# dV and dK stores of two attention backward passes: from GpSimd's DMA queue to SyncE's, in a fixed order with the K and V loads

## The chip, the cores and the metric

The kernel runs on one core of one Trainium2 chip, in bfloat16 with float32 accumulation. The metric is the device time of one execution in microseconds (us). Engines are called as the profile calls them: PE (TensorE), PEld (its weight loads), DVE (VectorE), ACT (ScalarE), POOL (GpSimd), SP (SyncE, which here only issues DMAs).

## The reference

Two independent attention blocks A and B, each with its own inputs, and the gradients of all of them for a given grad_out; the two outputs lie side by side in the last dimension.

```python
B, Sq, D = x.shape                     # 8, 96, 640
H, Dh = 32, 128                        # k_cache, v_cache: 8 x 32 x 512 x 128
q = (x @ wq).reshape(B, Sq, H, Dh).transpose(0, 2, 1, 3)
scores = einsum("bhqd,bhkd->bhqk", q, k_cache) * (Dh ** -0.5)
p = softmax(scores, axis=-1)
o = einsum("bhqk,bhkd->bhqd", p, v_cache)
out = o.transpose(0, 2, 1, 3).reshape(B, Sq, H * Dh) @ wo
...
# returned: out (A and B concatenated), then dx, dK, dV, dwq, dwo of A and of B
```

dK and dV have the size of the caches: 8 x 32 x 512 x 128 each, 33.5 MB, so four such outputs of 134.2 MB in all are written, and as much is read.

## The kernel before

The work goes in ticks. One tick starts one batch entry b of one head h of one block, so there are 2 x 32 x 8 = 512 of them, about 3.3 us each. What one (h, b) needs is spread over some 14 ticks as a software pipeline written out by hand: `em.add(tick, slot, function)` collects the pieces, they are sorted by tick and slot, and then recorded in that order. OFF gives the tick of each piece relative to the entry's own tick, SLOTS the place within a tick:

```python
OFF = dict(ldk=-5, ldv=-3, kt=-3, vt=0, s2=3, s3=3, s4=4, s5=5, s6=6, s7=7, s8=8)
SLOTS = dict(LOAD=0, S2A=5, S2B=5.5, S1=6, S8=10, S7=20, S5=30, S4=40, S6=50, S3A=52, S3B=53, S5B=54, HEAD=SL_HEAD, GRP=SL_GRP)
```

A scheduler of the language then may still move instructions on their engine by its own estimate, unless an instruction is wrapped in `pinned` (`tc.keep_in_program_order`): pinned instructions of one engine keep the recorded order among themselves.

The pieces around the change:

- `c_ld` (L262 to L270) loads K or V of two batch entries (a pair) at once, 256 KB, from SP. K_sb has 7 such buffers, V_sb 5. Not pinned.
- `c_xt` (L272 to L278) transposes such a pair on the way from SBUF to SBUF with a DMA transpose, also from SP: VT for every pair (4 buffers), KT for every second pair (2 buffers). For the other pairs PE transposes K itself (`c_s1`, L285). Not pinned.
- `c_s2a`, `c_s2b`, `c_s3a`, `c_s3b`: scores on PE (S_ps, L298), row maximum on DVE (L300), exponential on ACT (E_sb, L310), 1/sum on DVE (rinv, L320), product P_sb on POOL (L329, pinned).
- `c_s4` (L382 to L393): dV = P^T dO on PE (dV_ps, L389), evicted by ACT into dV_sb (L392), which holds two ticks and has 3 buffers. `c_s7` (L425 to L436): the same for dK (dK_ps L432, dK_sb L435).
- `c_st` (L395 to L399): when both ticks of a pair are evicted, one store of 256 KB from dV_sb or dK_sb to the output, issued from POOL and pinned there, one tick after the product, behind that tick's P_sb and prod.
- `c_s6` (L411): dP = dO V^T on PE, reading VT (L417), and dS on DVE (L421). `c_s8` and `c_s45` (L333 to L380): dQ, the transposes of dS and P, and O, with evictions by ACT (L375, L378).

Every eighth tick a head begins and another ends: its weights wq and wo are loaded from POOL (L190, L199), its projections are made on PE (L243) and its dwq and dwo are made and stored from POOL (L474, L496). After each group of up to 6 heads the partial out and dx are summed (`gU`, L512). At the border of A and B, x and grad_out of B are loaded from SP (ld_tmp, L118) and transposed on PE (L134).

Of the kernel before, what the change touches and what calls it, by code (L numbers as in the profile page):

```python
# [44 lines left out]
OFF = dict(ldk=-5, ldv=-3, kt=-3, vt=0, s2=3, s3=3, s4=4, s5=5, s6=6, s7=7, s8=8)  # L45
# [5 lines left out]
SLOTS = dict(LOAD=0, S2A=5, S2B=5.5, S1=6, S8=10, S7=20, S5=30, S4=40, S6=50, S3A=52, S3B=53, S5B=54, HEAD=SL_HEAD, GRP=SL_GRP)  # L51


def build_block(tc, em, tick0, blk, x, kc, vc, wq, wo, g_all, out_all, dx, dk, dv, dwq, dwo, ident, ones, pools, HG=6, first=True, groups=None):
    nc = tc.nc
# [7 lines left out]
    KC = Sk // 128  # L63
    NB = 2
# [38 lines left out]
    SB = {}  # L103
    HS = pools["HS"]
    CS = pools["CS"]
# [5 lines left out]
    def pinned(ins):  # L111
        return tc.keep_in_program_order(ins)
# [68 lines left out]
    def pA(h):  # L181
        def f():
            start = first and h == 0
            if h % 2 == 0:
                wq_p = hd.tile([128, DC, 256], BF16, name="wq_p", bufs=2)
                with nc.allow_non_contiguous_dma(reason="wq slice of two heads"):
                    if start:
                        nc.sync.dma_start(wq_p[:], wq_v[:, :, h * 128:(h + 2) * 128])
                    else:
                        pinned(nc.gpsimd.dma_start(wq_p[:], wq_v[:, :, h * 128:(h + 2) * 128]))  # L190
            else:
                wq_p = HS[(blk, h - 1)]["wq_p"]
            HS[(blk, h)] = dict(wq_p=wq_p, wq_h=wq_p[:, :, (h % 2) * 128:(h % 2 + 1) * 128])
        return f

    def pA2(h):
        def f():
            wo_h = hst.tile([128, D], BF16, name="wo_h", bufs=HG + 3)
            ld = nc.gpsimd.dma_start(wo_h[:], wo[h * 128:(h + 1) * 128, :])  # L199
            if not (first and h == 0):  # L200
                pinned(ld)
            HS[(blk, h)]["wo_h"] = wo_h
        return f
# [23 lines left out]
    def pC(h, which, si):  # L227
        def f():
            st = HS[(blk, h)]
            (t0, w) = tsplits[si]  # L230
            if which == 0:
                dst = st["QT_h"]
                lhs = lambda c: st["wq_h"][:, c, :]
                rhsT = S["xT"]
                sc = scale
            else:
                dst = st["dOT_h"]
                lhs = lambda c: st["woT_h"][:, c * 128:(c + 1) * 128]
                rhsT = S["gT"]
                sc = None  # L240
            q_ps = bank([128, w], F32, "q_ps")
            for c in range(DC):
                nc.tensor.matmul(q_ps[:], lhs(c), rhsT[:, c, t0:t0 + w], start=(c == 0), stop=(c == DC - 1))  # L243
            evac(EV["pC%d%d" % (which, si)], dst[:, t0:t0 + w], q_ps[:], sc)
        return f
# [16 lines left out]
    def c_ld(h, b, n, bufs):  # L262
        def f():
            src = kc if n == "K" else vc
            X = kvp.tile([128, NB, KC, 128], BF16, name=n + "_sb", bufs=bufs)
            nc.sync.dma_start(X[:], src[b:b + NB, h].rearrange("b (p c) d -> p b c d", c=KC))
            for i in range(NB):
                st = CS.setdefault((blk, h, b + i), {})
                st[n + "_sb"], st[n + "_all"] = X[:, i], X
        return f  # L270

    def c_xt(h, b, name, bufs):  # L272
        def f():
            XT = kvp.tile([128, NB * KC, 128], BF16, name=name, bufs=bufs)
            nc.sync.dma_start_transpose(XT[:], CS[(blk, h, b)][name[0] + "_all"][:].rearrange("p a c d -> p (a c d)"))
            for i in range(NB):
                CS[(blk, h, b + i)][name] = XT[:, i * KC:(i + 1) * KC].rearrange("p c k -> p (c k)")
        return f  # L278
# [116 lines left out]
    def c_st(h, b, which):  # L395
        def f():
            dst = dv if which == "v" else dk
            pinned(nc.gpsimd.dma_start(dst[b - 1:b + 1, h].rearrange("b (p c) d -> p b (c d)", c=KC), SB.pop((blk, h, b // 2, which))[:]))  # L398
        return f  # L399

    def c_s5b(h, b):
# [146 lines left out]
    def k_on_pe(h, b):  # L548
        return (b // NB) % 2 == 0 or h == 0 or (first and h == 1)

    SX = pools["SX"]
    for g in range(NG):
        h0 = GH0[g]
        for hh in range(groups[g]):
            h = h0 + hh
            c0t = tick0 + h * B
            if not (first and h == 0):
                em.add(c0t + HK["pA"], 54.6, pA(h))
                em.add(c0t + HK["pA2"], 54.6, pA2(h))
            em.add(c0t + HK["pB"], SL_HEAD, pB(h))  # L560
            fh = first and h == 0
            p0, p1, d1, d0, late = HK["pC0"], HK["pC1"], HK["pD1"], HK["pD0"], 0
            if fh:
                p1, d1, d0, late = [3, 3], 3, 4, 7
            elif h == 0:
                p0, p1, d1, d0, late = [-2, 2], [0, 3], 3, 4, 7
            for si in range(NTS):
                em.add(c0t + p0[min(si, 1)], SL_HEAD, pC(h, 0, si))
                em.add(c0t + p1[min(si, 1)], SL_HEAD + late, pC(h, 1, si))
            em.add(c0t + d1, SL_HEAD + (8 if late else 0), pD(h, 1))  # L570
            em.add(c0t + d0, SL_HEAD, pD(h, 0))
            for b in range(B):
                ct = c0t + b
                if b % NB == 0:
                    em.add(tick0 - 12 if first and h == 0 and b == 0 else ct + OFF["ldk"], SLOTS["LOAD"], c_ld(h, b, "K", 7))
                    em.add(ct + OFF["ldv"], SLOTS["LOAD"], c_ld(h, b, "V", 5))
                    if not k_on_pe(h, b):
                        em.add(ct + OFF["kt"], SLOTS["LOAD"] + 1, c_xt(h, b, "KT", 2))
                    em.add(ct + OFF["vt"], SLOTS["LOAD"] + 1, c_xt(h, b, "VT", 4))
                if k_on_pe(h, b):  # L580
                    em.add(ct + 2, SLOTS["S1"], c_s1(h, b))
                em.add(ct + OFF["s2"], SLOTS["S2A"], c_s2a(h, b))
                em.add(ct + OFF["s2"], SLOTS["S2B"], c_s2b(h, b))
                em.add(ct + OFF["s3"], SLOTS["S3A"], c_s3a(h, b))
                em.add(ct + OFF["s3"], SLOTS["S3B"], c_s3b(h, b))
                em.add(ct + OFF["s5"], SLOTS["S5B"], c_s5b(h, b))
                if b % 2 == 1:
                    em.add(ct + OFF["s4"] + 1, 54.3, c_st(h, b, "v"))
                    em.add(ct + OFF["s7"] + 1, 54.3, c_st(h, b, "k"))
                em.add(ct + OFF["s4"], SLOTS["S4"], c_s4(h, b))  # L590
                for i, o in enumerate(("s8", "s7", "s5", "s4")):
                    SX.setdefault(ct + OFF[o], [None] * 4)[i] = (blk, h, b)
                em.add(ct + OFF["s6"], SLOTS["S6"], c_s6(h, b))
                em.add(ct + OFF["s7"], SLOTS["S7"], c_s7(h, b))
            hk = HK if first or h < H - 1 else dict(HK, qA0=13, qB=[14, 15], qA1=16, qD=[(19, 0, 2), (19, 2, 4), (19, 4, 5)])
            em.add(c0t + hk["qA0"], SL_HEAD, qA(h, 0))
            for di in range(len(wsplits)):
                em.add(c0t + hk["qB"][di], SL_HEAD + 1, qB(h, di))
            em.add(c0t + hk["qA1"], SL_HEAD, qA(h, 1))
            for (k_, c_lo, c_hi) in hk["qD"]:  # L600
                if c_lo < DC and h % 2 == 1:
                    em.add(c0t + k_, SL_HEAD + 2, qD(h, c_lo, min(c_hi, DC)))
        cLg = tick0 + (h0 + groups[g] - 1) * B + B - 1
        gs0 = max(3, (GSPREAD0 * groups[g]) // HG)
        gs1 = max(3, (GSPREAD1 * groups[g]) // HG)
        if not first and g == NG - 2:
            gs0, gs1 = 9, 9
        if g == 0:
            em.add(cLg + OFF["s5"] - 2, SL_LOAD, setup_acc)
        subs = [(0, t, gi) for t in range(TT) for gi in range(len(gsplits))] + [(1, t, gi) for t in range(TT) for gi in range(len(gsplits))]  # L610
        n_out = TT * len(gsplits)
        for i, (which, t, gi) in enumerate(subs):
            if which == 0:
                tk = cLg + OFF["s5"] + 2 + (i * gs0) // n_out
            else:
                tk = cLg + OFF["s8"] + 2 + gs0 - 3 + ((i - n_out) * gs1) // n_out
            em.add(tk, SL_GRP, gU(g, which, t, gi))
# [124 lines left out]
```

## Time and profile before

| | |
|---|---|
| runs, median of 3 | 1705.34 us (1693.32 to 1706.98) |
| profiled execution, span from first to last instruction | 1699.8 us |
| PE busy | 1675.7 us (99%) |
| ACT, DVE, POOL busy | 1405.2, 1329.8, 1040.3 us |
| SP's queue (q1) | 242.08 MB in 546576 packets |
| POOL's queue (q0) | 177.35 MB in 53584 packets |
| stores of dV, of dK (POOL, L398) | 256 each, mean 761 and 762 ns on POOL; 5.2 and 5.3 us to landing |
| loads of K and V (SP, L266) | 512, 5.2 us to landing |
| transposes by DMA (SP, L275) | 256 of V, 122 of K, 5.8 us to landing |

Of the profiled execution the page gives the span, and no time from outside it; it lies within the range of the three runs. Busy time of an engine is the time in which it executes; for POOL it includes the issue of its DMAs, while all of SP's instructions count as issue or wait. "To landing" is the median from issue to the completion of the transfer. The share of a DMA queue is the time that its packets took, over 16 engines' span; packets of two queues on one engine can overlap in it, so shares can add to more than 100%.

### The profile page before, as it was taken

The page shows a single profiled execution, that of the slowest core. Times are in us where ns is not written, and L with a number is a line of the kernel's source. Part 1 is how long each engine was busy: PE and PEld are TensorE (multiplying, and loading weights), DVE is VectorE, ACT ScalarE, POOL GpSimd, SP SyncE. Part 2 cuts the span into 40 slices and gives each one's busy share as a digit, 9 for nine tenths or more (in the row PEclk, how much of TensorE's full clock was granted, in tenths as well). Part 3 has the DMA queues.
Part 4 walks back from the last instruction along what each step waited for, and adds up shares of the span by engine and source line. Part 5 has one row for each costly group of instructions (what it writes and reads, how often), then busy time and mean ns, then how long its engine had stood idle before and what let it go on. Part 6 is the DMA issues. An engine that isn't in the chain of part 4 may idle for free.

```text
span 1699.8 us, 56567 instructions
## 1 busy us (share of the span) xinstructions
PE 1675.7 (99%) x22024; PEld 1343.8 (79%) x22024; DVE 1329.8 (78%) x3052; ACT 1405.2 (83%) x3518; POOL 1040.3 (61%) x1747
## 2 busy tenths in 40 slices
PE   8999999999999999999999999999999999999999
PEld 7877778778778778777778877887788778778876
DVE  6887678878788878787778876787788778878877
ACT  6998889869869869878768998897799679878975
POOL 3676567646647647656566764675576557656754
PEclk9999999999999999999999999999999999999999
DMA  9999999999999999999999999999899989999994
GB/s 256 252 259 250 258 225 260 262 242 243 262 221 252 268 238 259 225 251 237 281 256 269 273 270 248 238 289 248 218 261 276 237 221 261 281 217 240 263 247 141
DMA packets 600429, 423.05 MB, mean 249 GB/s; under 512 B 419360, under 2 KB 557984, under 8 KB 600160
## 3 DMA queue, kind: packets, MB, share of 16 engines
q1 hardware_dynamic: 546576, 242.08, 72.2%
q0 software_dynamic: 53584, 177.35, 32.7%
q8 instruction: 173, 2.83, 0.7%
q14 instruction: 96, 0.79, 0.2%
HBM read 161.09 MB, written 159.12 MB: 188 GB/s over the span
## 4 chain that ended last, share of the span: by engine, by line
PE 89%; DMA 4%; ACT 3%; issue 1%; DVE 1%; POOL 0%; SPq 0%; DVEq 0%; ACTq 0%; POOLq 0%
PE q_ps L243 12%; PE o_ps L512 12%; PE dwo_ps L470 6%; PE dV_ps L389 6%; PE dK_ps L432 6%; PE S_ps L298 6%; PE dP_ps L417 6%; PE dwq_ps L490 6%; PE x_ps L340 5%; PE x_ps L365 5%; PE dst_ps L346 5%; PE x_ps L359 5%; PE kT_ps L285 3%; PE n_ps L258 3%; PE nat_ps L455 2%; DMA VT<-V_sb 1%
## 5 line engine op out<-in xcount | busy, mean ns | idle before, releaser
L329 POOL TENSOR_SCALAR P_sb<-E_sb,rinv 96x512 bf16<-96x512 bf16 x512 | 352.6, 689 | 567.8 <-DVE rinv L320 559.2
L310 ACT ACTIVATE E_sb<-S_ps,negm 96x512 bf16<-96x512 f32 x512 | 351.0, 686 | 187.6 <-DVE negm L300 181.9
L421 DVE SCALAR_TENSOR_TENSOR dS_sb<-dP_ps,dl_ps,P_sb 96x512 bf16<-96x512 f32 x512 | 382.1, 746 | 60.9 <-PE dl_ps L419 54.6
L300 DVE TENSOR_REDUCE negm<-S_ps 96x1 f32<-96x512 f32 x512 | 347.6, 679 | 50.9 <-PE S_ps L298 46.6
L435 ACT ACTIVATE dK_sb<-dK_ps 128x512 bf16<-128x512 f32 x512 | 302.1, 590 | 63.4 <-PE dK_ps L432 56.5
L392 ACT ACTIVATE dV_sb<-dV_ps 128x512 bf16<-128x512 f32 x512 | 311.6, 609 | 0.0
L378 ACT ACTIVATE PT_sb<-x_ps 128x384 bf16<-128x384 bf16 x512 | 253.1, 494 | 0.0
L512 PEld LDWEIGHTS <-OD 128*128 128x128 bf16 x1536 | 132.2, 98 | 100.4 <-issue 1.0
L398 POOL DMA_DIRECT2D out_dram<-dV_sb x256 | 194.9, 761 | 11.8 <-issue 8.6
L398 POOL DMA_DIRECT2D out_dram<-dK_sb x256 | 195.0, 762 | 9.1 <-issue 4.4
L389 PE MATMUL dV_ps<-dOnat_h,P_sb 96*128 96x128 bf16 x2048 | 198.2, 219 | 0.8 <-DVE dOnat_h L160 0.6
L417 PE MATMUL dP_ps<-VT,dOT_h 128*96 128x512 bf16 x512 | 195.4, 382 | 3.0 <-DMA VT<-V_sb 3.0
L432 PE MATMUL dK_ps<-Qnat_h,dS_sb 96*128 96x128 bf16 x2048 | 198.1, 219 | 0.1
L407 POOL TENSOR_TENSOR prod<-OD,dOT_h 128x96 bf16<-128x96 bf16 x512 | 184.2, 360 | 13.8 <-ACT OD L375 12.6
L348 DVE COPY dST_sb<-dst_ps 128x384 bf16<-128x384 bf16 x512 | 177.1, 346 | 10.5 <-PE dst_ps L346 10.3
L365 PE MATMUL x_ps<-ident,P_sb 96*128 96x96 bf16 x2048 | 172.0, 205 | 0.8 <-POOL P_sb L329 0.3
L359 PE MATMUL x_ps<-PT_sb,V_sb 128*128 128x96 bf16 x2048 | 172.3, 206 | 0.2 <-ACT PT_sb L378 0.2
L346 PE MATMUL dst_ps<-ident,dS_sb 96*128 96x96 bf16 x2048 | 172.3, 206 | 0.2 <-DVE dS_sb L421 0.2
L340 PE MATMUL x_ps<-dST_sb,K_sb 128*128 128x96 bf16 x2048 | 171.0, 206 | 1.3 <-ACT dK_sb L435 0.8
L375 ACT ACTIVATE OD<-x_ps 128x192 bf16<-128x192 f32 (+1 forms) x515 | 167.9, 326 | 3.9 <-PE x_ps L340 3.9
L320 DVE RECIPROCAL rinv<-rowsum 96x1 f32<-96x1 f32 x512 | 79.9, 156 | 106.0 <-ACT E_sb L310 100.4
L340 PEld LDWEIGHTS <-K_sb 128*128 128x128 bf16 x2048 | 131.1, 98 | 25.1 <-issue 1.6
(84 smaller groups left out, 3744.4 us busy)
## 6 DMA issues: line engine op xcount, KB each, us to landing
out_dram<-dV_sb POOLq DMA_DIRECT2D x256, 256.0 KB, 5.2
out_dram<-dK_sb POOLq DMA_DIRECT2D x256, 256.0 KB, 5.3
K_sb<-in_A_k_cache_dram SPq DMA_DIRECT2D x128, 256.0 KB, 5.3
V_sb<-in_A_v_cache_dram SPq DMA_DIRECT2D x128, 256.0 KB, 5.2
K_sb<-in_B_k_cache_dram SPq DMA_DIRECT2D x128, 256.0 KB, 5.0
V_sb<-in_B_v_cache_dram SPq DMA_DIRECT2D x128, 256.0 KB, 4.9
out_dram<-dwo_sb POOLq DMA_DIRECT2D x63, 160.0 KB, 4.8
out_dram<-dwq_sb POOLq DMA_DIRECT2D x31, 320.0 KB, 6.1
```

The source lines that it names most:

```text
L300: nc.vector.tensor_reduce(negm[:], S_ps[:], axis=AX.X, op=ALU.max, negate=True)
L310: nc.scalar.activation(E_sb[:], st["S_ps"][:], ACT.Exp, bias=st["negm"][:], scale=1.0, accum_out=rowsum[:])
L329: pinned(nc.gpsimd.tensor_scalar(P_sb[:], st["E_sb"][:], st["rinv"][:], 0.0, op0=ALU.mult, op1=ALU.add))
L340: nc.tensor.matmul(dQT_ps, st["K_sb"][:, c, :], st["dST_sb"][:, c * Sq:(c + 1) * Sq], start=(c == 0), stop=(c == KC - 1))
L389: nc.tensor.matmul(dV_ps[:, c * 128:(c + 1) * 128], P_sb[:, c * 128:(c + 1) * 128], hs["dOnat_h"][:, b * 128:(b + 1) * 128], start=True, s ...
L392: nc.scalar.activation(SB[(blk, h, b // 2, "v")][:, b % 2], dV_ps[:], ACT.Identity, scale=1.0)
L398: pinned(nc.gpsimd.dma_start(dst[b - 1:b + 1, h].rearrange("b (p c) d -> p b (c d)", c=KC), SB.pop((blk, h, b // 2, which))[:]))
L417: nc.tensor.matmul(dP_ps[:], hs["dOT_h"][:, tok], st["VT"], start=True, stop=True)
L421: nc.vector.scalar_tensor_tensor(dS_sb[:], dP_ps[:], dl_ps[:, 0:1], st["P_sb"][:], op0=ALU.subtract, op1=ALU.mult)
L432: nc.tensor.matmul(dK_ps[:, c * 128:(c + 1) * 128], dS_sb[:, c * 128:(c + 1) * 128], hs["Qnat_h"][:, b * 128:(b + 1) * 128], start=True, s ...
L435: nc.scalar.activation(SB[(blk, h, b // 2, "k")][:, b % 2], dK_ps[:], ACT.Identity, scale=1.0)
L512: nc.tensor.matmul(o_ps[:], src[:, t * 128:(t + 1) * 128], rhs, start=(hh == 0), stop=(hh == groups[g] - 1))
```

## The change

The stores of dV and dK are issued from SP. Their slot moves from 54.3 (late in the tick) to 1.5, behind the tick's loads (0) and DMA transposes (1) and ahead of the compute, still one tick after the product. The K and V loads and the transposes are pinned as well, so that SP issues all of these in the recorded order: in one tick V, K, KT (every second pair) and the store of dK, in the next VT and the store of dV.

```diff
@@ c_ld
-            nc.sync.dma_start(X[:], src[b:b + NB, h].rearrange("b (p c) d -> p b c d", c=KC))
+            pinned(nc.sync.dma_start(X[:], src[b:b + NB, h].rearrange("b (p c) d -> p b c d", c=KC)))
@@ c_xt
-            nc.sync.dma_start_transpose(XT[:], CS[(blk, h, b)][name[0] + "_all"][:].rearrange("p a c d -> p (a c d)"))
+            pinned(nc.sync.dma_start_transpose(XT[:], CS[(blk, h, b)][name[0] + "_all"][:].rearrange("p a c d -> p (a c d)")))
@@ c_st
-            pinned(nc.gpsimd.dma_start(dst[b - 1:b + 1, h].rearrange("b (p c) d -> p b (c d)", c=KC), SB.pop((blk, h, b // 2, which))[:]))
+            pinned(nc.sync.dma_start(dst[b - 1:b + 1, h].rearrange("b (p c) d -> p b (c d)", c=KC), SB.pop((blk, h, b // 2, which))[:]))
@@ build_block
                 if b % 2 == 1:
-                    em.add(ct + OFF["s4"] + 1, 54.3, c_st(h, b, "v"))
-                    em.add(ct + OFF["s7"] + 1, 54.3, c_st(h, b, "k"))
+                    em.add(ct + OFF["s4"] + 1, SLOTS["LOAD"] + 1.5, c_st(h, b, "v"))
+                    em.add(ct + OFF["s7"] + 1, SLOTS["LOAD"] + 1.5, c_st(h, b, "k"))
```

In the built programs the order on PE, DVE and ACT is the same as before. On SP the K transpose stood before directly behind the load that feeds it; now it stands behind the next pair's loads. The compiler gives each DMA of SP one of eight completion semaphores in turn, before and after, and a DMA waits until the earlier one on its semaphore has landed.

## The prediction

> **What bounds the kernel now.** I read the engine totals first, then what TensorE (PE) waited for, then the DMA queues and the same totals by stage, and last SyncE's (SP's) waits. From the page:
>
> ```profile
> span 1699.8 us, 56567 instructions
> PE 1675.7 (99%) x22024; PEld 1343.8 (79%) x22024; DVE 1329.8 (78%) x3052; ACT 1405.2 (83%) x3518; POOL 1040.3 (61%) x1747
> ```
>
> PE is busy in 1675.7 of 1699.8 us, so 24.1 us is all the idle time that any change around it can remove. The instruction order of the changed program is the same as before on PE, VectorE and ScalarE; GpSimd (POOL) loses 512 DMA issues and SP gains them. PE's work therefore stays 1675.7 us and only its idle time can move. What that idle time waits for, by the view of PE's waits:
>
> ```profile
> PE dP_ps L417 <- DMA VT<-V_sb: 3.0, 2, 2.4
> PE tp_ps L134 <- DMA ld_tmp<-in_grad_out_dram: 2.7, 1, 2.7
> PE S_ps L298 <- DMA KT<-K_sb: 2.1, 1, 2.1
> PE kT_ps L285 <- ACT dK_sb L435: 1.6, 1, 1.6
> ```
>
> Columns: us in total, times, longest. All DMA waits are a few us, so the transfers are hidden today. The DMA queues of the page show at what margin:
>
> ```profile
> q1 hardware_dynamic: 546576, 242.08, 72.2%
> q0 software_dynamic: 53584, 177.35, 32.7%
> ```
>
> Packets, MB, share of 16 engines' span. q1 is SP's queue (loads and transposes), q0 POOL's (stores, weights). They add to 104.9%: there is hardly a moment without packets in flight, though over 100% says that packets of the two queues overlap, so the share is not pure work. The view by stages (PE, PEld, DVE, ACT, POOL busy, granted clock, DMA share, GB/s):
>
> ```profile
> 250.00:350.00 100.00, 99.75 (x1338) 80.89 (x1336) 80.94 (x186) 86.84 (x218) 65.05 (x111) 1.00 1.14 256
> 650.00:750.00 100.00, 99.31 (x1319) 79.49 (x1317) 80.74 (x186) 83.01 (x209) 62.68 (x105) 1.00 1.14 240
> 1150.00:1250.00 100.00, 99.62 (x1267) 78.12 (x1265) 77.87 (x181) 76.83 (x191) 56.72 (x95) 1.00 0.96 236
> ```
>
> Of the sixteen 100 us stages from 50 to 1650 us, seven have a DMA share of 1.11 or more, the lowest has 0.96. PE is the bound, and DMA is a close second, kept off the path by prefetch. Pairing each V transpose with the dP matmul that reads it (k-th transpose, matmul 2k-1), it lands 11.9 us ahead in the median, but 2.7 us or less ahead in one of twenty, mostly near 100 to 170, 690 to 730 and 970 to 1010 us. That reserve is what the change draws on or refills.
>
> **What leaves POOL.** 512 issues of 0.76 us (page, L398: 194.9 + 195.0 us). POOL falls to about 650 us. POOL's P_sb (L329) waits 559.2 us for rinv in 404 of 512 cases, so in most ticks it was idle when its input came, and PE waits for P_sb 0.3 us in all (2.0 us at its weight loads). Value: 0, bounds 0 and -2 us. What hides the lost 390 us is that idle time itself: POOL was no bound.
>
> **What SP gains.** I price a store's issue by the K and V loads on the same queue, which have the same size and shape (128 partitions, 256 KB): medians 474 to 615 ns, mean of the four 0.53 us, so 512 x 0.53 = 271 us. SP issues today 512 x 0.53 + 256 x 1.44 (V transposes) + 122 x 1.25 (K) = 793 us, later 1064 us, 63% of the span. A pair of ticks takes (1669.2 - 12.2) / 256 = 6.5 us (first and last S_ps matmul); per pair SP then issues for 4.2 us. It fits, with 2.3 us for waits, where it had 3.4.
>
> **The waits on SP.** Each store waits for ScalarE's eviction of the tick before. Behind it in the order stand the V transpose or the next pair's loads. Those wait themselves for PE work of the tick before to free a buffer, so a store's wait ends about when theirs do: value 0; bounds 0 and, for a dV store that comes after the eviction ending a tick, the 0.6 us of that eviction (L392) x 256 = 154 us on SP, spent from the reserve above and not on PE. In exchange the fixed order takes this away:
>
> ```profile
> SPq L266 <- PE dK_ps L432: 180.0, 102, 4.2
> SPq L275 <- DMA K_sb<-in_A_k_cache_dram: 169.4, 57, 9.0
> SPq L275 <- DMA K_sb<-in_B_k_cache_dram: 152.0, 61, 4.8
> ```
>
> Today a K transpose stands right behind the load that feeds it and blocks SP until that lands, 321 us in 118 waits. In the new order it stands two ticks later, behind the next pair's loads, and a store parts it from the V transpose. So loads behind it leave earlier. There is one more wait: the program has eight completion semaphores for SP's DMAs, taken in turn, so a DMA must have landed before the eighth one after it is issued. Per pair SP had 890 / 256 = 3.5 DMAs and will have 5.5: the limit moves from 15 us to 8 / 5.5 x 6.5 = 9.5 us. Landing medians are 5.2 (loads, L266) and 5.8 us (transposes, L275); the longest are 14.4 and 14.9, so it binds in the crowded stages only.
>
> **The transfers.** The bytes stay, the packets change. q0 averages 177.35 MB / 53584 = 3.3 KB a packet; the packets between 512 B and 2 KB, 557984 - 419360 = 138,624 by the page, are SP's plain DMAs, about 256 of 1 KB for each of 512 loads, and a store from SP has the same rows. The tail of the trace has each kind alone, stores from POOL in 1676 to 1686 us and stores from SP in 1686.5 to 1699.8 us:
>
> ```profile
> q0 software_dynamic: 368, 1.21, 31.7%
> ```
>
> ```profile
> q1 hardware_dynamic: 2528, 2.46, 53.2%
> ```
>
> 0.317 x 10 x 16 = 50.7 engine-us for 1.21 MB, 41.9 ns per KB; 0.532 x 13.3 x 16 = 113.2 for 2.46 MB, 46.0 ns per KB. The 512 stores carry 134.2 MB: 4.1 ns x 134,200 / 16 = 34 us more on all sixteen engines. It reaches the path only where DMA has no room: 7 of 16 stages, 15 us. Bounds: 0 (prefetch takes it all) and 34 us, plus what is lost if one queue cannot overlap transfers as two do, at most the 4.9% above 100%, 83 us.
>
> [...]
>
> **The gain.** With K's landing out of SP's way, the PE waits for VT (3.0) and KT (2.1) and the two behind a store's landing (1.6 above, 0.8 at L340) can go: 7.5 us. Bounds: 0 and the whole 24.1 us. I take 7.5, since the blocking that makes loads late is removed everywhere.
>
> **The sum.** 1699.8 + 15 - 7.5 = 1707.3 us. The page gives the profiled execution's span and no other time for it; the span lies 5.5 us under the median of the runs (1705.34; 1693.32 to 1706.98), so I put the 7.5 us on the median: 1713 us, +0.4%. Runs of this kernel lie 0.8% apart, so about 1% is what a measurement can tell from no change.
>
> **Rivals.**
>
> *Slower: the store's landing holds ScalarE.* dV_sb and dK_sb have three buffers of two ticks. A pair's buffer is stored in the third tick and written again in the seventh, four ticks or 13 us later. The trace has this happening once, after a late landing:
>
> ```profile
> 794.86 0.60 ACT L435 ACTIVATE dK_sb<-dK_ps 128x512 bf16<-128x512 f32 x1 [1.79 <-DMA out_dram<-dK_sb]
> ```
>
> ```profile
> 795.50 0.38 PE L285 MATMUL kT_ps<-ident,K_sb 128*128 128x128 bf16 x4 [1.65 <-ACT dK_sb L435]
> ```
>
> ScalarE waits 1.79 us for the store of that buffer and PE loses 1.65. In the new order a store also queues behind transposes and loads, on SP and in the ring. If one ring serves 34 us more work and loses half of the overlap (41 us), with the 7.5 us gain not coming, that is +75, 1780. If only the seven crowded stages pay and the gain still comes, 75 x 7 / 16 - 7.5 = +25, 1731. Centre 1755. It decides once a store lands more than 13 us after its eviction in the seven crowded stages. For: 1.11 to 1.14 shares there, landings up to 14.9 us. Against: only two such waits on ScalarE now (3.1 us), landing median 5.3.
>
> *Faster: the ring gets smoother.* A store from SP in the tail lands 1.8 us after issue (160 KB), from POOL 2.5 at least (256 KB). If packets cost the same in traffic, the 34 us vanish and most of the 24.1 us idle goes, less what start and end keep: about -18, 1687. For: no more K-landing block. Against: PE's waits for VT, KT and ld_tmp are only 8.7 us (3.0, 2.1, 2.7 and 0.9).
>
> *Nothing moves.* That stores stay on POOL is ruled out by the built order; that both effects hide wholly gives 1705.
>
> **Chances.** Forecast (within 1%, nothing moving included) 0.43; slower rival 0.40; faster rival 0.17. The range takes 1684 (3 us short of losing all 24.1 us) to 1768, midway between the slower rival's centre and its upper end; the forecast's own is 1697 to 1722.
>
> **What would show it.** Right: PE busy near 1676; POOL near 650; q0 down to about 43 MB and q1 up to 376 MB with some 131,000 more packets; the K_sb row gone from SP's waits; a few us in "ACT <- DMA out_dram". Wrong: tens of us in that row or in S_ps and dP_ps on KT and VT (slower), or PE idle under 10 us (faster).

## The result, and the profile after

| | before | after |
|---|---|---|
| median of the runs, us | 1704.81 (15 runs, 1692.10 to 1717.71) | 1685.62 (15 runs, 1683.96 to 1688.83) |
| ratio, 95% interval | | 0.9893 [0.9869, 0.9917] |
| profiled execution, span | 1699.8 | 1682.2 (its own time 1683.96) |
| PE busy, idle in the span | 1675.7, 24.1 | 1669.7, 12.5 |

The changed kernel is 1.1% faster. The forecast was +0.4%, within 1%. Ratios, here and below, are taken over all fast runs, those within 1.5% of the fastest of their kernel, so they differ a little from the quotient of two medians.

The totals of the page after, first the engines, then the two DMA queues (packets, MB, share of 16 engines' span):

```profile
span 1682.2 us, 57193 instructions
PE 1669.7 (99%) x22024; PEld 1340.7 (80%) x22024; DVE 1329.0 (79%) x3052; ACT 1403.0 (83%) x3518; POOL 665.7 (40%) x1235
...
q1 hardware_dynamic: 685840, 376.33, 93.1%
q0 software_dynamic: 12624, 43.10, 7.9%
```

The 17.6 us that the span lost are 11.6 us less idle time and 6.0 us less busy time on PE, with the same 22024 matmuls. The bytes moved as forecast, and q1 has 139,264 packets more (131,000 forecast). The queues' shares add to 101.0%, where they were 104.9%.

The longest of PE's waits after (us in total, times, longest):

```profile
PE warm_ps L658 <- DVE warm L645: 1.1, 1, 1.1
PE q_ps L243 <- ACT gT L157: 0.6, 1, 0.6
PE dV_ps L389 <- DVE dOnat_h L160: 0.6, 1, 0.6
PE q_ps L243 <- DVE gT L160: 0.6, 1, 0.6
```

All four rows shown of before are gone: VT, ld_tmp, KT, and ScalarE's dK_sb. Between 20 and 1650 us, PE idled 16.4 us before and 5.0 us after; some 7.5 us lie at the start and the end in both. The three stages that were shown before:

```profile
250.00:350.00 100.00, 99.89 (x1331) 80.45 (x1330) 79.84 (x184) 84.77 (x214) 40.90 (x76) 1.00 1.06 260
...
650.00:750.00 100.00, 99.94 (x1323) 79.76 (x1322) 81.63 (x189) 82.90 (x209) 40.05 (x74) 1.00 1.03 256
...
1150.00:1250.00 100.00, 99.64 (x1301) 79.58 (x1298) 78.98 (x181) 78.24 (x196) 35.92 (x67) 1.00 0.96 227
```

The DMA share, last column but one, fell from 1.14 to 1.06 and 1.03 in two of these stages. It did not fall everywhere: the highest of the sixteen stages is 1.14 after too (50 to 150 us, 1.13 before). SP's waits after:

```profile
SPq L266 <- PE dK_ps L432: 312.8, 165, 4.6
...
SPq L398 <- ACT dV_sb L392: 46.3, 91, 3.7
...
SPq L398 <- ACT PT_sb L378: 36.2, 76, 1.3
```

The K_sb rows (321 us) are down to 1.6 us. The stores (L398) wait for ScalarE instead. The first row of the K and V loads (L266) grew from 180.0 us; all their waits for PE together grew little, from 464 to 488 us. How the V transposes land is at the end of the view of the tile VT, before and then after:

```profile
DMA to landing us min/median/max: 3.1/6.1/14.9
```

```profile
DMA to landing us min/median/max: 3.1/4.9/10.4
```

Pairing each of the 378 transposes in the trace with the first matmul that reads it gives the reserve (landed so long before use). Before, it is under 3 us for 33 of them and zero for the worst; after, for none, with 3.7 us the least.

**Why busy time fell too.** This is the first late V transpose of before in PE's timeline (start, us, instruction, and in brackets the wait ahead of it), then the stretch behind it by windows (us, busy PE, PEld, DVE, ACT, POOL, granted clock, DMA share, GB/s):

```profile
125.33 0.39 PE L417 MATMUL dP_ps<-VT,dOT_h 128*96 128x512 bf16 x1 [2.37 <-DMA VT<-V_sb]
...
126.81 2.55 PE L490 MATMUL dwq_ps<-dQnat,x_nat 128*128 128x256 bf16 x11
```

```profile
127.00:128.00 1.00, 1.00 (x7) 0.73 (x5) 0.85 (x2) 0.05 (x1) 0.00 (x0) 0.50 1.08 262
...
130.00:131.00 1.00, 1.00 (x23) 1.00 (x21) 0.74 (x4) 0.46 (x1) 0.40 (x1) 1.00 0.85 59
...
829.00:833.00 4.00, 4.00 (x43) 3.38 (x42) 2.46 (x7) 2.46 (x6) 1.73 (x3) 0.59 1.15 251
```

PE waits 2.37 us, then runs at a granted clock of 0.50 from 126.6 to 130.0 us. The wait for ld_tmp (2.74 us) at 826 us was followed by 3.4 us of half clock as well (0.59 in the mean from 829 to 833 us). So these two waits are paid twice: their 6.8 us at half clock cost PE about 3.4 us of the 6.0 (an estimate, half of 6.8). The trace of after has none of it between 20 and 1650 us. Instruction by instruction (the order is the same), 1.8 us of the 6.0 lie from 100 to 150 us, 1.7 from 800 to 850 and 1.4 in the first 50 us; the last are not explained.

So late transposes are not all of the 17.6 us. They account for 5.1 us of waits (VT 3.0, KT 2.1) and about 1.7 us of half clock; x and grad_out of B (ld_tmp) for 3.6 us (2.7 and 0.9) and 1.7; ScalarE's buffers, held by stores, for 2.4 (1.6 and 0.8). What they share is a transfer that lands late.

One profiled execution is one of many, but the record has the mean granted clock of every run. Of the 97 runs of before beside the experiments, the 4 with 1.000 took 1695.9 us in the mean, the 24 with 0.998 took 1703.4 and the 16 with 0.995 took 1713.4 (correlation of time and clock over all 97: -0.75). All 15 runs of after had 0.999 or 1.000. So the scatter of before goes with half clock that differs from run to run, but even its runs at full clock are some 10 us slower than after.

### The profile page after: what moved, and what is told of

Read it like the earlier page. It is cut to its first block, busy times and chain, and to the rows that moved or that the text cites. A ratio compares the mean times of both kernels' runs of the same rounds, so it can differ in the third digit from the quotient of the medians.

```text
span 1682.2 us, 57193 instructions
## 1 busy us (share of the span) xinstructions
PE 1669.7 (99%) x22024; PEld 1340.7 (80%) x22024; DVE 1329.0 (79%) x3052; ACT 1403.0 (83%) x3518; POOL 665.7 (40%) x1235
## 4 chain that ended last, share of the span: by engine, by line
PE 93%; ACT 3%; DVE 1%; issue 1%; DMA 1%; POOL 0%; SPq 0%; DVEq 0%; ACTq 0%; POOLq 0%
PE q_ps L243 13%; PE o_ps L512 12%; PE dwo_ps L470 7%; PE dK_ps L432 6%; PE dV_ps L389 6%; PE S_ps L298 6%; PE dwq_ps L490 6%; PE dP_ps L417 6%; PE x_ps L340 5%; PE dst_ps L346 5%; PE x_ps L365 5%; PE x_ps L359 5%; PE kT_ps L285 3%; PE n_ps L258 3%; PE nat_ps L455 2%
## 5 line engine op out<-in xcount | busy, mean ns | idle before, releaser
L359 PE MATMUL x_ps<-PT_sb,V_sb 128*128 128x96 bf16 x2048 | 172.1, 206 | 0.5 <-ACT PT_sb L378 0.5
L243 PE MATMUL q_ps<-gT,woT_h 128*128 128x512 bf16 (+1 forms) x640 | 136.9, 325 | 1.2 <-ACT gT L157 0.6
L470 PE MATMUL dwo_ps<-g_nat,Onat 128*128 128x320 bf16 x768 | 135.2, 298 | 1.6 <-ACT E_sb L310 0.2
```

## Experiments

All times are ratios to runs of the kernel before on the same chip. "DMA time" is the sum of the queues' shares (q0, q1 and, in e7, ScalarE's q10) times the span; "reserve < 3" counts transposes; "K wait" is SP's wait for a K load to land (L275 on K_sb). The last three are worked out from one profiled execution. Those of after, e1 and e6 are among the fastest of their kernel (1683.96, 1719.71 and 1685.65 us).

| kernel | stores on | median, us | ratio [95%] | DMA time, us | reserve < 3 | K wait, us |
|---|---|---|---|---|---|---|
| before | POOL | 1704.81 | 1 | 1783 | 33 | 321 |
| after | SP | 1685.62 | 0.9893 [0.9869, 0.9917] | 1699 | 0 | 2 |
| e1 pins only | POOL | 1727.34 | 1.0128 [1.0096, 1.0161] | 1793 | 24 | 116 |
| e2 stores only | SP | 1687.49 | 0.9891 [0.9867, 0.9914] | 1752 | 0 | 95 |
| e4 POOL kept busy | SP | 1688.05 | 0.9893 [0.9872, 0.9915] | 1700 | 0 | 3 |
| e5 dV only | half | 1687.08 | 0.9866 [0.9831, 0.9901] | 1735 | 2 | 47 |
| e6 dK only | half | 1691.08 | 0.9927 [0.9896, 0.9959] | 1723 | 0 | 18 |
| e9 pins, KT early | POOL | 1709.66 | 0.9975 [0.9941, 1.0009] | 1775 | 29 | 329 |
| e11 all earlier | POOL | 1715.24 | 1.0035 [0.9997, 1.0072] | 1694 | 15 | 44 |
| e13 K and KT early | POOL | 1738.30 | 1.0162 [1.0115, 1.0210] | 1810 | 34 | 0 |
| e14 K and KT early | SP | 1685.82 | 0.9888 [0.9856, 0.9920] | 1732 | 0 | 0 |
| e3 KT early | SP | 1708.87 | 1.0018 [0.9992, 1.0043] | 1780 | 0 | 180 |
| e8 e3, dK_sb x4 | SP | 1710.45 | 1.0006 [0.9977, 1.0036] | 1788 | 0 | 183 |
| e10 e8, dV_sb x4, V_sb x4 | SP | 1715.49 | 1.0053 [1.0019, 1.0086] | 1808 | 73 | 201 |
| e12 e3, store first | SP | 1694.85 | 0.9923 [0.9892, 0.9955] | 1761 | 0 | 162 |
| e7 stores on ScalarE | ACT | 1797.74 | one run | 1735 | – | 11 |

### Queue, order or POOL's time: e1, e2, e4

After reading the two traces there were three theories: A, the fixed order (SP no longer blocked by K landings); B, the queue of the stores (their place in the tick moves with it); C, POOL's 390 us.

e1 undoes the move of the stores and keeps the pins:

```diff
-            pinned(nc.sync.dma_start(dst[b - 1:b + 1, h]...
+            pinned(nc.gpsimd.dma_start(dst[b - 1:b + 1, h]...
-                    em.add(ct + OFF["s4"] + 1, SLOTS["LOAD"] + 1.5, c_st(h, b, "v"))   # and dK alike
+                    em.add(ct + OFF["s4"] + 1, 54.3, c_st(h, b, "v"))
```

> The K and V loads and the DMA transposes are pinned in the fixed order on SP as in the change; the stores of dV and dK stay on POOL as before. Theory A (order): the gain comes from taking the K transpose away from behind its own load, where it blocked SP for 321 us in 118 waits; then this alone gives most of the gain, 1684 to 1692 us, and the waits of SP for K_sb's landing are gone. Theory B (queue): the gain comes from the stores leaving POOL's queue, since transfers of two queues disturb each other; then this stays at 1698 to 1706 us, with PE still waiting a few us for VT or KT. In either theory POOL stays near 1040 us.

e2 moves the stores and leaves loads and transposes unpinned:

```diff
-            pinned(nc.sync.dma_start(X[:], src[...]))     # c_ld; c_xt alike
+            nc.sync.dma_start(X[:], src[...])
```

> The stores go to SP as in the change, but loads and transposes are not pinned, so the scheduler orders them against the pinned stores by its own estimate; the K transpose stands one load nearer to its own K load than in the change. Theory A: SP again waits for K_sb's landing, in part; time between, 1688 to 1700 us. Theory B: the whole gain, 1684 to 1688 us, POOL near 666 us.

e4 gives POOL its time back by making P_sb a second time into an unused tile:

```diff
+                em.add(ct + OFF["s3"], 54.3, lambda h=h, b=b: pinned(nc.gpsimd.tensor_scalar(wk.tile([Sq, Sk], BF16, name="junk", bufs=2)[:], ..., op0=ALU.mult, op1=ALU.add)))
```

> The changed kernel with POOL's freed time filled again: in every tick, where a store was issued before, POOL makes P_sb a second time into a scratch tile (512 times about 0.69 us, 353 us in all). If POOL's time was part of the gain (theory C), this is 4 us or more slower than the changed kernel; if POOL was no bound, as the prediction had it, it is within 2 us of 1685.6, with POOL near 1020 us.

The order alone makes the kernel 1.3% slower, which neither theory had expected; the stores alone give the whole gain; and with POOL busy again for 1002.6 us the ratio stays (the median is 2.4 us above after's, 2 were expected at most). A and C fell. Where e1 loses, by PE's waits:

```profile
PE S_ps L298 <- DMA KT<-K_sb: 20.1, 5, 6.6
```

Five late K transposes cost 20.1 us, and all five are followed by half clock, 27.3 us in all. The order of after puts the K transpose a tick later, and with the stores on POOL that is too late for it.

### Half the stores: e5, e6

```diff
-            pinned(nc.sync.dma_start(dst[b - 1:b + 1, h]...
+            pinned((nc.sync if which == "v" else nc.gpsimd).dma_start(dst[b - 1:b + 1, h]...   # e6: "k"
```

The half left on POOL goes back to slot 54.3.

> Half the dose: the 256 dV stores are issued from SP, the 256 dK stores from POOL at their old place; loads and transposes pinned as in the changed kernel. Theory B (what the stores cost on POOL's queue is what the change removes): DMA time, the two queues' shares times the span, falls about half way from the pins-only run's (70.8+33.6)% x 1717.9 = 1794 us to the changed kernel's (93.1+7.9)% x 1682.2 = 1699 us, to about 1746, with q0 near 43 + 67 = 110 MB and the reserve of the V and K transposes between the two kernels'. If the time follows the DMA time linearly it is half way from 1727.3 to 1685.6, about 1706; if TensorE only loses where the reserve reaches zero (a threshold), most of the loss goes with the first half: 1688 to 1696. Rival D (it is the dV store's place between the V transposes in SP's order that helps, not the queue): all of the gain, 1686, with DMA time unchanged near 1790.

> The other half of the stores: the 256 dK stores are issued from SP, the 256 dV stores from POOL at their old place. Theory R (reserve: the stores on POOL's queue make every landing later; half of them moved is enough to keep the V and K transposes ahead of their matmuls): as with the dV stores alone, DMA time near 1735 us and 1687 us, within 3 us. Rival D (the dV store's place between the V transposes is what helps): no gain from dK alone, DMA time near 1785 and 1705 to 1727.

The dV half gives all of the gain, the dK half some two thirds of it (1691.08 us, 1 us over what theory R expected; its interval touches after's). DMA time is about half way (1735 and 1723 us), but the ratio is not: PE has no wait for VT or KT in either profiled execution. This looks like a threshold, as a reserve that either holds or doesn't would make it. In e6 it doesn't hold in every run: the profiled execution is one of its fastest, with a granted clock of 1.000, and its two slowest runs, 1700.1 and 1700.4 us, had 0.997. The dV store's place between the V transposes isn't needed for most of the gain. The longest landing of a V transpose fell in step, 17.3 us in e1, 12.1 in e5, 10.6 in e6.

### The place of the K transpose: e9, e3

With `OFF["kt"] - 1` the K transpose stands one tick earlier, at its place before the change, right behind the load that feeds it; e9 has the stores on POOL, e3 on SP.

```diff
-                        em.add(ct + OFF["kt"], SLOTS["LOAD"] + 1, c_xt(h, b, "KT", 2))
+                        em.add(ct + OFF["kt"] - 1, SLOTS["LOAD"] + 1, c_xt(h, b, "KT", 2))
```

> Stores on POOL, loads and transposes pinned, the K transpose one tick earlier than in the pins-only run (1727.3 us): nearly the order of the kernel before, written out. It fills the fourth cell of stores on POOL or SP by K transpose early or late. If the place has one price whatever the queue (+23 us from 1685.6 to 1708.9 with stores on SP): 1727 + 23 = 1750. If the early place only hurts through stores queued behind it on SP, and gives the K transposes back the reserve that the pins-only run lost (its S_ps waits on KT, 20.1 + 21.8 us, gone): about 1705, as the kernel before. In both cases DMA time should stay near 1785 us, since the stores are on POOL's queue.

> The changed kernel with the K transpose one tick earlier, directly behind the V transpose that follows its K load, the place it had before the change; stores stay on SP. Theory A: SP waits for K_sb's landing again by 200 us or more, loads start late, and most of the gain is lost: 1697 to 1706 us. Theory B: within 3 us of the changed kernel, 1684 to 1689 us.

The place has opposite signs on the two queues. With stores on POOL it helps (1.0128 to 0.9975, which is the kernel before again); with stores on SP it costs the whole gain (0.9893 to 1.0018), although every transpose of e3 keeps 5.0 us of reserve or more. What e3 waits for, on ScalarE and then on PE:

```profile
ACT dK_sb L435 <- DMA out_dram<-dK_sb: 14.3, 19, 1.9
...
ACT dV_sb L392 <- DMA out_dram<-dV_sb: 9.4, 9, 2.2
```

```profile
PE dst_ps L346 <- ACT dV_sb L392: 3.4, 4, 1.3
PE kT_ps L285 <- ACT dK_sb L435: 2.5, 5, 0.7
PE S_ps L298 <- ACT dK_sb L435: 2.5, 2, 1.4
```

SP stands 180 us in waits for K landings with the stores queued behind:

```profile
SPq L275 <- DMA K_sb<-in_A_k_cache_dram: 91.9, 57, 3.4
SPq L275 <- DMA K_sb<-in_B_k_cache_dram: 88.4, 59, 3.3
```

The stores leave late: in the median a dV store is issued 5.1 us after the eviction that fills its buffer (1.8 in after), a dK store 5.4 us (3.5). ScalarE is then held by their buffers. This is the mechanism of the prediction's slower rival; the change as made doesn't trigger it (0.8 us on ScalarE).

### Is the held ScalarE all of e3's loss: e8, e10, e12, e14

e8 has a fourth buffer for dK_sb, e10 one for dV_sb too (V_sb gives up one of five), e12 puts the store ahead of the tick's loads and transposes (slot -0.5 for 1.5).

> The run with the K transpose one tick earlier (1708.9 us), with a fourth buffer for dK_sb. Theory (the store's landing holds ScalarE: the K transpose blocks SP until its load lands, the dV and dK stores behind it leave late, and ScalarE waits for their buffers 14.3 us on dK and 9.4 us on dV): ScalarE's waits on dK stores go to about 0, those on dV stay near 9 or grow as the hold-up moves there, and the time falls to about 1695 to 1700. Rival (the block of SP costs through something else, such as late loads): the ScalarE row goes but the time stays near 1709.

> The K transpose one tick earlier with stores on SP (1708.9 us), now with a fourth buffer for both dV_sb and dK_sb (V_sb gives up one of its five to make room). A fourth buffer for dK_sb alone took ScalarE's 14.3 us of waits on dK stores away but raised those on dV stores from 9.4 to 24.3. Theory (late stores holding ScalarE are the whole loss): both rows gone, 1686 to 1692. Rival (SP, blocked by the K transpose's wait for its load, falls behind by more than any buffer holds, or loads come late): the wait shows up elsewhere on PE and the time stays above 1700.

> The K transpose one tick earlier with stores on SP (1708.9 us), buffers as there, but in each tick the store stands ahead of the loads and transposes instead of behind them, so that the K transpose, which waits for its load to land, no longer stands between an eviction and its store. Theory (in that run the loss is ScalarE waiting for late stores, 14.3 + 9.4 us): both of ScalarE's rows on stores fall under 3 us, the reserve of the transposes stays above 3 us, and the time is 1686 to 1693. Rival (SP has no time left with the K transpose's waits of 180 us in it, wherever the store stands; the hold-up moves into the loads and transposes behind the store): the rows on stores fall, but PE waits on VT, KT or loads appear, and the time stays above 1700.

e8 missed: the dK row went, but the hold-up moved to dV and the time stayed:

```profile
ACT dV_sb L392 <- DMA out_dram<-dV_sb: 24.3, 17, 4.3
```

e10 tells nothing: V_sb is also read by PE (L359) until nine ticks after its load, so with four buffers of two ticks each the V loads had to be late, and 73 transposes had a reserve under 3 us. e12 got 14 of the 23 us back, 2 us short of what was expected. The dV row fell under 3 us, the dK row didn't, and PE still waits for dK_sb in the rows on kT_ps, S_ps and x_ps:

```profile
ACT dK_sb L435 <- DMA out_dram<-dK_sb: 8.8, 9, 2.6
...
ACT dV_sb L392 <- DMA out_dram<-dV_sb: 1.9, 3, 1.0
```

e14 removes the cause instead. K loads and K transposes both go a tick earlier, with an eighth K_sb buffer, so that the transpose is as early as in e3 but its load is two ticks old:

```diff
-OFF = dict(ldk=-5, ldv=-3, kt=-3, vt=0, ...
+OFF = dict(ldk=-6, ldv=-3, kt=-4, vt=0, ...
-                    ... c_ld(h, b, "K", 7))
+                    ... c_ld(h, b, "K", 8))
```

> The changed kernel with the same edit: K loads and K transposes one tick earlier, one more K_sb buffer, stores on SP. The K transpose is as early as in the run of 1708.9 us, but its load is two ticks old, so it does not wait for a landing ahead of the stores. Theory (that run lost by the wait for the K landing, which made the stores late and held ScalarE): no K_sb row among SP's waits, ScalarE's waits on stores under 3 us, 1685 to 1690. Rival (the early place itself is bad, since the transposes crowd the stores in the queue): ScalarE's rows on stores above 8 us and 1695 or more.

0.9888, the time of after; no K_sb row among SP's waits, 5.6 us of ScalarE on dV stores (more than the 3 expected). So it was the wait for the landing that cost e3 its time, most of it through the stores behind it (e12), and not the early place. The edit also starts the K loads earlier and adds a buffer; no run separates these from the wait that they remove. e14 is also no better than after: with no late transpose, more reserve for the K transposes buys nothing.

### Can order make the reserve with the stores on POOL: e11, e13

e11 moves K loads, K and V transposes a tick earlier than e1 (K_sb 8, VT 5, V_sb 4 buffers). e13 is e1 with the edit of e14.

> All stores stay on POOL; instead the reserve is made by earlier issue: in the pinned order K loads and K transposes go one tick earlier than in the pins-only run, and V transposes one tick earlier (eight K_sb and five VT buffers for seven and four, V_sb four for five), so that no K transpose stands right behind its load. Theory R (before loses only where a transpose lands after its matmul is ready; the DMA time in itself is no bound): PE's waits on VT and KT are gone, 1686 to 1694, though DMA time stays near 1785 us. Rival P (the 84 us of DMA time are the gain itself): DMA time near 1785 and 1700 or more, whatever the order.

> The pins-only run (stores on POOL, 1727.3 us) with K loads and K transposes one tick (3.3 us) earlier and one more K_sb buffer; V loads and all other buffers as there, and no transpose stands behind its own load. Its only large waits were S_ps on KT, 20.1 us on PE, with 27.3 us of half clock; the reserve of the K transposes there had a smallest value of 0.0 and a 5% point of 0.1 us. Theory R (time is lost only where a transpose lands late; the queue matters through that alone): the 5% point rises to about 3 us, the KT waits fall under 5 us, half clock under 10 us, and the time to 1693 to 1704, that is 23 to 34 us less than the pins-only run. Rival Q (the stores' queue costs in itself, and landings stretch with whatever lead they are given): landings grow, KT or VT waits stay above 10 us, and the time stays at 1710 or more.

Both missed, and in e11 the rival too (its DMA time fell). e11 has the fault of e10, four V_sb buffers: its loads (L266) waited 513.6 us on SP for PE to free one. e13 has no such fault and is the slowest of all with stores on POOL. Its waits, on PE:

```profile
PE dP_ps L417 <- DMA VT<-V_sb: 16.0, 8, 5.2
PE S_ps L298 <- DMA KT<-K_sb: 14.2, 5, 5.0
```

The K transposes were issued earlier (the shortest lead from issue to use rose from 4.7 us in e1 to 7.9), but they landed later; the view of the tile KT, e1 and then e13:

```profile
DMA to landing us min/median/max: 3.3/5.7/13.8
```

```profile
DMA to landing us min/median/max: 3.4/6.6/16.8
```

So theory R fell in the form in which it was put: with the stores on POOL's queue, the earlier issue was eaten by longer landings (6.6 us in the median for 5.7), and the V transposes paid as well (16.0 us of PE's waits in e13). The three orders on POOL with five V_sb buffers go the same way: the less SP is held by K landings (329, 116, 0 us), the slower the kernel (0.9975, 1.0128, 1.0162; the last two intervals overlap). e11 (44 us, 1.0035), with four, is off that line. On SP it is the reverse (180, 162, 2 and 0 us: 1.0018, 0.9923, 0.9893 and 0.9888), though the 95 us of e2, in shorter waits, cost nothing. The fixed order pays only together with the move.

### A second hardware queue: e7

```diff
-            pinned(nc.sync.dma_start(dst[b - 1:b + 1, h]...
+            pinned(nc.scalar.dma_start(dst[b - 1:b + 1, h]...
```

> The stores are issued from ScalarE instead of SP, so they travel on a second hardware queue beside SP's; the place in the order is that of the changed kernel. Read for the DMA price, not for the time: ScalarE gains 512 issues of about 0.5 us (256 us on top of 1405 us busy), which brings it level with PE, so the time is expected to be worse than 1700, up to 1760. Theory B1 (POOL's kind of queue is dear in traffic): DMA time near 1700 us as in the changed kernel and landings of stores near 4 us. Theory B2 (any second queue in flight beside the transposes is dear): DMA time near 1780 us as before, landings near 5.

1735 us of DMA time lies between the two theories' numbers, in traffic thinned by a kernel that is 5% longer. The V transposes' landing, 5.3 us in the median and 12.2 at most, lies between before and after too, and the stores land in 4.2 and 4.1 us, as from SP. It does not decide. The time, 1797.74 us, is worse than the 1760 that were expected at most, and by another way: ScalarE is busy for only 79%, and PE idles for work of ScalarE, VectorE and POOL that comes late.

## Why the prediction was wrong

**The step that failed first: "The transfers".** It priced packets in the tail, where each queue was alone, at 41.9 ns per KB for POOL's and 46.0 for SP's, made 34 us more DMA time of it, and put 15 on the path. Measured, DMA time fell by 84 us (1783 to 1699), and on PE the term is 0: the only wait for a DMA that is left is 0.5 us for x_nat at the start.

The ranking that the tail gave wasn't wrong. In the packet records of before, POOL's packets over 2 KB took 49.5 ns per KB and SP's of about 1 KB 51.3; after, SP's of that size, now loads and stores together, took 48.2. What the step left out is that the transfers beside the stores change with them: the transposes' packets (those under 512 B on q1, without the 8192 that the stores bring) took 12,316 engine-us before and about 11,640 after, and there are as many. If loads and stores of after took the same per KB, then some 42 of the 84 us are the transposes', 27 the loads' and 11 the stores' (an estimate from these rates). Nor is the time in flight a price that reaches the path: e2 has 1752 us of it and is as fast as after with 1699, e11 has 1694 and is slow. The 84 us are a sign of the traffic, not the gain.

**The second: "The gain".** It took 7.5 us of waits; 11.6 us of idle and 6.0 of busy time went. The rows that it counted did go, and ld_tmp's 2.7 us besides, which it had left out. The 6.0 it could not contain, since it said that "PE's work therefore stays 1675.7 us": the half clock behind two of the waits was in the trace, at 126.6 and 829.7 us. The view by stages that it read shows it too, in two stages that it didn't print:

```profile
50.00:150.00 100.00, 97.50 (x1358) 81.53 (x1356) 80.54 (x185) 90.74 (x230) 67.73 (x114) 0.98 1.13 255
...
750.00:850.00 100.00, 92.82 (x1251) 76.26 (x1249) 77.53 (x180) 77.21 (x195) 57.18 (x96) 0.98 1.13 263
```

With 150 to 250 us (97.85 busy), these two hold 11.8 of the 16.4 us of idle time as well. The prediction's reserve also covers the V transposes alone; of the K transposes, one in twenty landed about 1 us or less ahead. It also gave the wrong reason: "the blocking that makes loads late is removed everywhere". e1 removed two thirds of that blocking and e13 all of it, with the stores on POOL, and both were slower.

**The bound on SP.** A store of 0.53 us was right (medians 0.538 and 0.532 us). SP waited 201 us for ScalarE with its stores (all rows of L398; the five largest are 46.3, 36.2, 31.3, 28.4 and 18.0), more than the 154 us that were given as the far bound, and PE saw none of it. POOL's term of 0 was right (e4), POOL fell to 665.7 us, and the K_sb rows went.

**The rivals.** The faster one (1687), which was given the least chance, 0.17, is what was measured, 1685.62; the forecast's own range, 1697 to 1722, doesn't hold it. Its mechanism, "the ring gets smoother", stands as far as landings go; its condition, that packets cost the same in traffic, nearly does (49.5 and 48.2 ns per KB). Its weight was cut by "Against: PE's waits for VT, KT and ld_tmp are only 8.7 us", which leaves out the half clock again. Its mark, PE idle under 10 us, was set too low: 7.5 us of the 12.5 lie at start and end. The slower rival is real but needs SP blocked ahead of a store (e3), not more bytes on one queue.

The stores' median landing fell with the move, from 5.2 and 5.3 us (dV and dK, from POOL) to 4.0 and 4.4 us (from SP).

**What stays open.** Shown is that moving the stores off POOL's queue makes the gain, without the new order (e2) and without POOL's time (e4); that with all stores on POOL's queue transfers land late (V transposes before 6.1 us in the median and 14.9 at most, after 4.9 and 10.4); that moving half of them brings most of the gain; and that no order tried mends it with the stores left there. Why they land late is not settled. It may be POOL's kind of queue, or any second queue beside the transposes; e7, with 5.3 us in the median for the V transposes, does not decide. A third reading has no run at all: the moment of issue moves with the queue, since all stores on POOL stand at slot 54.3 and none at 1.5. In the median a dV store leaves 2.9 us after its eviction before and 1.8 after, a dK store 3.9 and 3.5; and from SP it takes its turn between loads and transposes, while POOL issues it beside them.

## What to carry to other kernels

When PE is 99% busy and its DMA waits are a few us, look at how late the latest transfers land, at every stage with a granted clock under 1.00, and at the clock just behind each wait, in windows of 1 us: two waits of before, 2.37 and 2.74 us, were each followed by 3.4 us at a granted clock of 0.50. Price a transfer in the traffic in which it will run, with what it does to the transfers beside it (the transposes' packets fell from 12,316 to about 11,640 engine-us with nothing changed in them), and don't take a price per byte to the end: with half the stores moved, DMA time was about half way (1735 and 1723 us) and the gain all or two thirds of the whole (e5, e6). Look at what waits for a landing ahead of a store that is put on the loads' queue: 180 us of such waits on SP cost e3 the whole gain (1.0018), and without them e14 had it (0.9888); the 95 us of e2, in shorter waits, cost nothing.

## What the runs showed of the hardware

**The clock fell behind most gaps of 2.1 us or more.** In the traces of before, after and e1 to e14, between 20 and 1660 us, PE has 28 gaps of 2.1 us or more. With 22 of them the granted clock falls to 0.5, within the gap or up to 2 us behind it (or is there already, once in e13), for 3.4 us or a multiple of it (in before from 126.56 to 129.97 and from 829.71 to 833.12 us); the shortest of these was 2.12 us (e8). Six are not followed (2.15 and 2.33 us in e13, 2.30 in e8, 2.36 in e5, 3.04 in e11, 3.57 in e14), and of eleven gaps from 1.6 to 2.1 us two are. Once, at 565.3 us in e7, the clock fell with no gap over 1.5 us near it; PE was busy for 3.41 of the 5 us before.

**An earlier issue landed later.** With the stores on POOL, K transposes issued a tick earlier (e13) took 6.6 us in the median where in e1 they had taken 5.7.
